# Halving the filler products of TensorE's first waits, and a newly written order of issue, in a block-recurrent attention and feed-forward kernel

## Chip, cores and metric

The kernel runs on one NeuronCore of one Trainium2 chip, as a single launch. The metric is device time in microseconds (us). The engines are named as the profile names them: PE (TensorE matmul), PEld (TensorE weight load), DVE (VectorE), ACT (ScalarE), POOL (GpSimd) and SP (SyncE, which here only issues DMAs).

## What is computed

```python
# x: (8, 8, 512, 64), state: (8, 8, 32, 64), both f32
scores = scale * x @ state.T                  # per batch and head, 512 x 32
xread  = softmax(scores, -1) @ state          # 512 x 64
scores2 = scale * state @ x.T                 # 32 x 512
sread  = softmax(scores2, -1) @ x             # 32 x 64
a = concat([xread, sread], axis=2)            # (8, 8, 544, 64)

t = a.transpose(0, 2, 1, 3).reshape(4352, 512)
h = t @ w_in                                  # 512 -> 2048
g = h * erf(softplus(h))
out = g @ w_out                               # 2048 -> 512
```

## The kernel before

Everything is f32. A batch (block) `b` has 512 tokens (its x rows) and 32 state rows. The feed-forward part is run in two halves `u` of the 2048 hidden columns. The product of the attention weights with the state and then with `w_in` is regrouped: state times `w_in` is formed first (`mixed`, L836), and the attention weights are applied to that (`first_product`, L935). First and second products use seven-product schemes in place of eight, some of them twice nested (L935, L1019, L1255), whose sums run on DVE (L975, L986, L1237) and whose copies out of PSUM run on ACT (L947, L1265).

Block 0 is done apart, while the weights still arrive (functions ending in `0`): eight heads of x are loaded by four DMAs (`load`, L395), transposed (`turn`, L410), scored (`score`, L436), the scores turned (`turn_score`, L442), and a softmax runs on DVE and ACT (L461 to L471) for two groups `g` of four heads. The attention weights are turned back (`turn_a`, L446) and copied into the tile `aT` (`either("ta0")`, `either("ta1")`). `mixed0` (L586) forms state times `w_in` for one or two column groups, and its result is copied into the tile `m`. `first0` (L604) is the first product of block 0: two matmuls of 128x512 that sum over the two groups, `es` 0 and 1; for block row `i` = 0 of the first half they were already two operations of one matmul each (`split`), for the others one operation of two. `second0` (L629) is the second product. In the same stretch the weights are loaded into three `raw` buffers and converted by `convert`: two ACT passes (L548, L550) and three DVE passes (L552, L554, L556) for each pair of 128-column groups. After a `raw` buffer is free, SP loads the next pair into it.

Query tiles for the later blocks are loaded by `load_xq` (16 DMAs of 64 KB, L93), transposed on DVE (L684) and scored on PE (L692). The x rows are loaded by `load_x_static` (4 DMAs of 256 KB, L783).

Nothing is issued as it is written. Each piece of work is recorded by `op(engine, cost, at, go, reads, writes, ...)`, with a cost in us, a due time `at`, and for DMAs a transfer time `pipe` and a time to landing `land`. At the end `emit` takes, for each engine, an order written out by hand as numbers in the table `ORDER` (number k is the k-th operation recorded for that engine). It computes when each would begin by the costs, and issues them all sorted by that begin. `in_order` then ties each engine to that order. So what stands on an engine one behind the other is set by `ORDER`; the costs, `land` and `pipe` only set how the engines' lists are merged. An engine never overtakes in its own list: an operation that waits holds up all behind it.

`either(name, ...)` puts a small copy on DVE if its name is in the set `BY_VECTOR`, and on ACT if not.

`spare_products(name, n, at)` records `n` filler products: `warm` (L115) multiplies the 128x128 identity by itself into a PSUM bank that is not in use. Their results are never read. They lie between the operations of block 0, where TensorE would wait. Including the eight at the very start (operation 0, `begin0`), the program has 78 of them. Each is recorded in the profile as two MATMUL rows, as every f32 product that is not a transpose is.

```python
def spare_products(name, n, at):
    op(PE, 0.112 * n, at, lambda: warm(bank(name)[:, 0:P], n), [], [name])
```

Of the kernel before, what the change touches and what calls it, by code (L numbers as in the profile page):

```python
# [17 lines left out]
def kernel(  # L18
# [21 lines left out]
    P = 128  # L40
# [99 lines left out]
    def op(engine, cost, at, go, reads=(), writes=(), table=None, land=0.0, pipe=0.0):  # L140
# [14 lines left out]
        x0 st s00 ta0 m001 m010 m011 m020 u1 m120""".split())  # L155

    def either(name, cost, out, in_, at, reads, writes):
# [3 lines left out]
        else:  # L161
# [4 lines left out]
            0 8 5 1-3 6 4 9 7 10 12 15-16 21 17 22 18 25 19 13 23 11 24 14 26-29 20 31 33 32 53 30  # L166
            45 68 52 44 69 71 34 54 36 35 37 70 39 47 38 40 55 57 56 48-49 73 58-59 50 41 61 42 46
            51 63 72 43 76-77 92 78 74 79 81 80 62 82 85 60 83 75 84 88 64 87 89 93 86 65 90 66 94
            91 67 95 101 96-97 105 102 106 98 130 129 103-104 107-108 132 131 109 133 110-111 134
            136 112 135 138-139 113 137 140 114-115 141 117 99 143 116 118 142 100 121-122 119  # L170
            123-124 120 144 146 125-127 176 148-149 152-153 128 179 178 150-151 180 154 177 181 183
            182 155-156 186 160-161 187 185 157-158 184 188 162-163 189 159 145 190 147 164 191 193
            168-169 165 224 170-171 223 166-167 226 225 195 227 172-174 230 196-198 228-229 199 233
            200 232 175 201 234 211 202 207 203 231 212 235 204 192 237 208 236 194 205-206 209 238
            240 210 270 213-216 271 217-218 272-273 242 239 243-244 274 245 219-220 275 250 276
            221-222 251 277 246 258 254 252 280 255-256 247-248 281 278-279 282 253 241 283 249 259
            284-285 257 287 286 260 262 317 263-264 261 320 265 319 318 266-268 289-290 269 291 321
            292 288 324 322 297-298 323 327 293 326 325 299 328 300-302 294-295 329 303 305-306 330
            296 304 332 331 333 309-310 363 307 364 311-312 308 366 335 365 367 313-314 336 315 370
            334 368 316 369 373 342 372 343 345 344 374 371 338 346 337 376 347 339 348 375 340 356  # L180
            341 357 405 358 349 359-360 407 351 361 353 362 406 350 352 384 409 386 385 355 388 387
            354 377 389 408 390 378-379 411-412 381 380 382 398 413 383 414 400 391 402 410 415 393
            392 417 394-395 416 418 399 401 433-434 397 396 439-440 437 441 435 403 442 436 404 438
            443 423 444-446 419 424 421 448 447 420 431 463 422 429 464 427 466 432 425 467 465 430
            426 468 428 470 453 449 473 469 451 472 471 474 454 450 475-476 452 459 457 460 477-478
            455 458 507 461 456 462 508 510 479 486 509 511 487 480 512 488 482 514 490 481 513 483
            489 517 516 484-485 492 518 515 491 493 520 500 495 519 522 521 501 494 502 497 496
            551-552 503-504 553-554 499 506 558 505 555 530 498 556 523 531-532 524 557 561 560 525
            559 533 562 527 534 563 535 526 564 528 565-566 536 529 595 544 537 545 539 547 546 538
            548 597 549 541 540 598 550 596 574 599 542 576 543 602 578 600 567 575 579 577 568 601  # L190
            569 605 603 570 606 571 607 572 604 580 608 588 573 609-610 581 589 591 590 583 640 639
            582 592 642 593 585 594 641 643 584 618 586-587 619-621 611 644 613 646 615 622 645 623
            612 649 648 647 614 624 650 632 617 652 616 651 625 633 654 653 634 627 635 683 636 626
            637 629 628 685-686 684 630 687 631 638 655 688 662 656 690 657 663-665 692-693 666 689
            694 659 658 668 691 660 695 667 696 676 697-698 661 727 678 677 669 679 670 672 680 671
            681-682 673 730 674 728 731 675 729 732 706 699 707 709 708 700 710 733 711 701-702 734
            703 735 737 704 712 736 738 720 705 739 713 740 722 715 721 724 723 741-742 714 725 716
            771 717 726 718 773-774 750 719 752 751 775 743 772 776 754 753 778 745 744 777 755 780
            756 781 747 782 779 746 748 783-784 764 749 765 757 766-767 759 758 761 760 768 762-763
            770 785 769 786-788 792 789 793 795 791 794 790 799 796 801 800 797-798 803 802 806  # L200
            804-805 808 807 813 809-810 815 814 816-817 811-812 818-819""",
        ACT: """
            0-3 5 4 11-12 6 13 7 14 8 31 16 15 9 17-18 55 20 10 56 19 32-34 36 38 21-22 37 39 24 23
            35 40-41 25-26 43 42 44-45 27-28 47 50 49 46 48 29 51 61 53 52 54 57-60 65 64 66-67
            94-95 68 102 104 103 70 107 69 106 71 98-99 72 77 63 96-97 79 76 73-74 78 80 75 86-87 81
            100 84 101 85 82 135 83 134 136-137 90 138-139 105 91 30 92 88 93 89 149 145 112 108 113
            151 150 62 152-153 158 142 140 159-160 141 161 146 109 143 162 155 147 157 144 165 163
            171 154 172 156 164 166 148 167 176 175 174 114 168 173 110 169 186 170 188 177 189 187
            190 182 195 179-180 111 115 178 197-198 196 192 200-201 194 118 184 199 191 193 203 202
            208 181 209 116 211 210 213 212 121 183 117 119-120 204 223 205 185 225 206 224 226 207  # L210
            227 232 215 123 234 214 122 219 216 233 217 125 124 126 235 229 236 245 127 130 218 230
            238 231 246 131 228 247 249 248 239 221 250 220 129 260 240 237 241-244 128 261-262 222
            253-254 256 263-264 133 252 269 132 251 271-272 268 270 274 266 273 265 275-276 255
            282-283 267 285 277 286 258 287 284 278 297 279-281 257 259 299 290 298 291 289 288 300
            293 301 306 308 294 292 309 307 310 305 303 313 304 302 311 295 322 321 319 314 312
            315-316 320 317 344 296 318 346 345 347 324 348 353 329 355 354 350 356 330 351 323 332
            325 331 326 352 327 349 333 357 361 360 328 339 358-359 362-363 340 334 341-342 364 335
            337 365 343 386 336 371-372 374 373 338 366-367 375 388 369-370 368 381 389 382 376 392
            377 390 379 378 387 393 384 399 401 394 391 395-396 383 385 380 402 397-398 405 403 407
            406 400 404 414 412-413 415 417 408-411 419 418 420-421 426 423 425 428-429 427 432 424  # L220
            422 430 433 431 434-436 439 437 442 441 440 463 438 416 465 448 443 464 466 449 467 472
            445 444 451 446 470 473 450 468 474-475 477 469 452 447 453 476 458 488 480 471 479 454
            485-486 478 487 459 481 509 482-483 455-456 461 460 510-511 484 512 462 457 494 513 518
            489 495 519 490 520 514 521 497 496 492 516 524 522 498 491 517 526 523 532-533 531 493
            525 515 534 504 555 499 527-528 500 505 529 506-507 530 502 501 557 508 556 540 558 541
            543 559 564 503 535 561 566 536 560 537 567 563 538 568 544 562 542 571 570 565 569 539
            572 550 573-574 579 578 580 545 577 551 575 546 576 552 601 553 548 554 603-604 547 586
# [3 lines left out]
            663 636 631 664 669 662 670 642 665 671 637 672 643 666 693 667 644-645 638 668 640 639  # L231
            646 695 641 696 694 678 673 697 679 681 674 698 701-702 675-676 680 682 699 704 677 703
            705 700 706 688 708-709 683 707 710 689 711 691 712 684 715 690 713 718 716-717 685-686
            692 739 714 687 724 741 725 742 740 727 719-720 743 726 748 745 750 744 746 751 722 747
            754 749 721 728 752-753 755 723 734 756-757 729 758-759 730 735 760 732 736 731 737 733
# [1255 lines left out]
    for i in range(2):  # L1491
        first0(0, i, "h%d" % i, 19 + 1.8 * i, split=not i)
# [220 lines left out]
```

## Time and profile before

| what | value |
|---|---|
| median of 3 runs | 710.77 us (709.85 to 713.2) |
| the profiled execution: its time / its span | 709.41 us / 707.6 us |
| TensorE clock granted, mean | 0.998 |
| HBM moved | 92.88 MB, mean 131 GB/s |
| DMA share, 10 to 20 / 20 to 30 / 30 to 40 us | 0.93 / 0.36 / 0.96 |

How to read it. The span runs from the first to the last instruction of the profiled execution; its time has 1.8 us more around it. Busy time of PE is a union of matmul rows whose ends are modelled, so PE can be reported as 100% busy when its rows are issued at a slower pace; start-to-start times within a group of like products are the safer reading. Since a filler product is a matmul as any other, the busy share of PE counts it as work. In the timeline a row is a run of like instructions on one engine: start, length, engine, line, operation, out<-in, and how many; brackets hold the idle time before it and what ended that.

### The profile page before, as it was taken

What the parts mean: (1) busy time and instruction counts of PE and PEld (TensorE: products, weight loads), DVE (VectorE), ACT (ScalarE), POOL (GpSimd) and SP (SyncE); (2) the same over time, 40 slices, a digit from 0 to 9 for tenths busy, and PEclk for the clock granted to TensorE, in tenths of its full rate; (3) what the DMA queues carried; (4) which work ended last, traced back from release to release, by engine and by line L of the source; (5) the groups of instructions that cost most, each with busy time, mean ns of one, the idle gap of its engine ahead of it and who ended that gap; (6) DMA issues with size and microseconds to landing.
All of it is one profiled execution on the core that took longest, in us unless ns stands there. A gap on an engine that the chain in (4) does not pass through costs nothing.

```text
span 707.6 us, 13386 instructions
## 1 busy us (share of the span) xinstructions
PE 698.9 (99%) x5259; PEld 592.3 (84%) x5259; DVE 593.9 (84%) x989; ACT 468.3 (66%) x847; POOL 85.6 (12%) x93
## 2 busy tenths in 40 slices
PE   9999989999999999999999999999999999999997
PEld 8734658787878878899999788898989898998996
DVE  5799989999999999797945589597969596959797
ACT  5797887868679393757335574759584757575832
POOL 0001010100111010000100100002242124122222
PEclk9999999999999999999999999999999999999999
DMA  8675969595969855413542720216385425555275
GB/s 272 159 195 127 224 183 198 186 222 160 220 162 253 257 204 153 151 74 82 119 112 79 236 67 31 68 16 113 46 128 63 95 24 104 75 60 61 30 135 105
DMA packets 133742, 92.88 MB, mean 131 GB/s; under 512 B 93744, under 2 KB 120752, under 8 KB 133168
## 3 DMA queue, kind: packets, MB, share of 16 engines
q1 hardware_dynamic: 114336, 61.88, 32.2%
q0 software_dynamic: 18800, 29.63, 22.7%
q8 instruction: 41, 0.67, 0.4%
q10 hardware_dynamic: 544, 0.52, 0.2%
q14 instruction: 21, 0.17, 0.1%
HBM read 50.86 MB, written 41.16 MB: 130 GB/s over the span
## 4 chain that ended last, share of the span: by engine, by line
PE 83%; DVE 6%; SPq 2%; issue 1%; DMA 0%; ACT 0%; DVEq 0%
PE o L1255 28%; PE h L935 17%; PE o L1019 17%; PE at L935 7%; PE o L1438 3%; PE h L1389 2%; PE h L836 2%; PE at L836 2%; SPq L93 2%; PE o L629 1%; DVE ring L986 1%; PE at L1389 1%; PE at L798 1%; DVE ring L1187 1%; PE h L692 1%
## 5 line engine op out<-in xcount | busy, mean ns | idle before, releaser
L947 ACT COPY ring<-h 128x512 f32<-128x512 f32 x120 | 68.8, 586 | 82.0 <-PE h L935 72.6
L935 PE MATMUL h<-aT,m 128*128 128x256 f32 x360 | 91.4, 380 | 0.0
L975 DVE TENSOR_TENSOR ring<-ring 128x1024 f32<-128x1024 f32 (+1 forms) x64 | 73.0, 1153 | 18.0 <-ACT ring L972 17.8
L1019 PE MATMUL o<-w_out,ring 128*128 128x256 f32 x320 | 77.2, 381 | 0.0
L957 ACT ACTIVATE ring<-ring 128x512 f32<-128x512 f32 x120 | 71.8, 631 | 6.9 <-DVE ring L953 3.9
L935 PEld LDWEIGHTS h<-aT,m 128*128 128x128 f32 x360 | 65.4, 190 | 9.4 <-issue 1.0
L986 DVE TENSOR_TENSOR ring<-ring 128x1024 f32<-128x1024 f32 x60 | 72.7, 1219 | 0.3
L1255 PE MATMUL o<-w_out,w_in 128*128 128x128 f32 x512 | 69.6, 277 | 0.3 <-DVE ring L1280 0.2
L1019 PEld LDWEIGHTS o<-w_out,ring 128*128 128x128 f32 x320 | 59.9, 190 | 10.8 <-issue 1.2
L1255 PEld LDWEIGHTS o<-w_out,w_in 128*128 128x128 f32 x512 | 64.1, 192 | 3.3 <-DVE oo L1270 1.1
L1255 PE MATMUL o<-w_out,ring 128*128 128x128 f32 x480 | 64.5, 276 | 0.0
L1255 PEld LDWEIGHTS o<-w_out,ring 128*128 128x128 f32 x480 | 61.1, 192 | 2.3 <-DVE ot L1270 0.4
L972 ACT ACTIVATE ring<-ring 128x1024 f32<-128x1024 f32 (+1 forms) x64 | 62.8, 1004 | 0.2
L1019 PE MATMUL o<-raw,ring 128*128 128x256 f32 x240 | 58.8, 382 | 0.0
L1019 PEld LDWEIGHTS o<-raw,ring 128*128 128x128 f32 x240 | 44.9, 190 | 10.7 <-issue 3.4
L1255 PE MATMUL o<-raw,ring 128*128 128x128 f32 x360 | 49.1, 275 | 0.0
L1255 PEld LDWEIGHTS o<-raw,ring 128*128 128x128 f32 x360 | 45.6, 192 | 1.8 <-issue 0.8
L1255 PE MATMUL o<-raw,xT 128*128 128x128 f32 x320 | 42.1, 276 | 0.0
L1255 PEld LDWEIGHTS o<-raw,xT 128*128 128x128 f32 x320 | 39.0, 192 | 1.4 <-issue 0.8
L1175 POOL DMA_DIRECT2D out_dram<-oo x16 | 23.6, 1548 | 116.7 <-DMA out_dram<-oo 93.9
L629 PE MATMUL o<-w_out,ring 128*128 128x512 f32 x64 | 31.2, 602 | 0.8 <-DVE ring L620 0.7
L935 PE MATMUL at<-aT,sx 128*128 128x256 f32 x120 | 31.0, 381 | 0.2 <-DVE ring L949 0.2
(270 smaller groups left out, 1418.4 us busy)
## 6 DMA issues: line engine op xcount, KB each, us to landing
x<-in_x_dram SPq DMA_DIRECT2D x30, 256.0 KB, 5.0
xq<-in_x_dram SPq DMA_DIRECT2D x112, 64.0 KB, 2.5
out_dram<-oo SPq DMA_DIRECT2D x10, 512.0 KB, 3.4
raw<-in_moe_w_in_dram SPq DMA_DIRECT2D x8, 512.0 KB, 6.2
raw<-in_moe_w_out_dram SPq DMA_DIRECT2D x4, 1024.0 KB, 7.5
raw<-in_moe_w_out_dram POOLq DMA_DIRECT2D x8, 512.0 KB, 4.7
raw<-in_moe_w_in_dram POOLq DMA_DIRECT2D x8, 512.0 KB, 5.4
kept_a<-aT SPq DMA_DIRECT2D x8, 512.0 KB, 4.8
```

Source lines behind the costliest of these rows:

```text
L629: nc.tensor.matmul(out=bank("o%d" % r), lhsT=gT[g][:, i, P * r:P * r + P], rhs=w_out[:, GF * g + i, :], start=(made_of[r] == 1), stop=(mad ...
L836: nc.tensor.matmul(out=bank(names[k])[Ns * p:Ns * p + Ns, :], lhsT=st[r, b, q], rhs=of_group[2 * u + j][r, :, i, :], start=True, stop=True)
L935: nc.tensor.matmul(out=out_[:, i], lhsT=x_[:, q:q + P], rhs=y_, start=(start and i == 0), stop=(i == 1), skip_group_check=not start)
L947: op(ACT, 0.5, t, lambda: nc.scalar.copy(out_(), view(bank(name))), [name], w)
L957: op(ACT, 0.53, t, lambda: nc.scalar.activation(out=part(splane, k), in_=part(hplane, k), func=ACTF.Softplus), area(hplane, ks=[k], os=[o] ...
L972: op(ACT, 0.085 + 0.875 * share, at + n, lambda s_=s_: nc.scalar.activation(out=s_, in_=s_, func=ACTF.Erf), [], area(splane, ks=[k], os=os ...
L975: op(DVE, 0.065 + 1.075 * share, at + n + 1, lambda s_=s_, h_=h_: tt(s_, s_, h_, op=ALU.mult), area(hplane, ks=[k], os=os), area(splane, k ...
L986: op(DVE, 1.14, at + k, lambda k=k, x_=x_, y_=y_, how=how: tt(get("h", k), get(*x_), get(*y_), op=how), area(v[x_[0]], ks=[x_[1]]) + area( ...
L1019: nc.tensor.matmul(out=view(name)[:, h], lhsT=lhs[:, i, :], rhs=weight_of[n]()[:, u, i, :], start=(start and h == 0 and i == 0), stop=(h = ...
L1175: op(GP, 1.2, t, lambda: nc.gpsimd.dma_start(out=quad(r, c), in_=one(v), accum_op=ALU.add), every(*v), [("out", b, r, c)], land=3.0, pipe=2.0)
L1255: nc.tensor.matmul(out=out_[:, Q2 * k:Q2 * k + Q2], lhsT=lhs[:, k, i], rhs=rhs[:, i], start=first, stop=(k == len(ns) - 1 and i == 1), ski ...
L1389: nc.tensor.matmul(out=bank(bk)[:, P * i:P * i + P], lhsT=x_[:, i, k], rhs=y_[:, k], start=(start and i == 0 and k == 0), stop=(i == GF - ...
```

## The change

Five edits are made together.

1. The cost that the planner is told for one filler product goes from 0.112 to 0.224 us, and there are fewer of them: 14 become 6 and 3 become 2 in `begin0`; the eight groups of 6 become eight groups of 3. With the two groups that stay (3 and 2) and the eight at the start, 78 products become 45.
2. `first0` of the first half is split by `es` for block row `i` = 1 too: one more operation of PE, the same matmuls. The first two block rows are now four operations.
3. The planner is told later landings: `land=4.0` in place of 2.5 for the x rows of a later block, and `land=6.0` for its query tiles. No DMA is added or removed.
4. Ten names stand in `BY_VECTOR` as before, but other ones: `st`, `ta0`, `m001`, `m010` and `u1` go to ACT, `x2`, `ta1`, `m000`, `m021` and `m121` to DVE.
5. All five lists of `ORDER` are written anew.

```diff
     BY_VECTOR = set("""
-        x0 st s00 ta0 m001 m010 m011 m020 u1 m120""".split())
+        x0 x2 s00 ta1 m000 m011 m020 m021 m120 m121""".split())
...
     ORDER = {
         PE: """
-            0 8 5 1-3 6 4 9 7 10 12 15-16 21 17 22 18 25 19 13 23 11 24 14 26-29 20 31 33 32 53 30
...
+            0-1 5 2-3 6 4 8-9 7 15 22-23 17 16 12 24-25 18 10-11 19 13-14 20 26-30 21 34 33 45 31-32
...
         SP: """
-            1 0 2 5-10 4 21 3 18 17 11-12 14 13 22-23 15 24 19 16 20 25-26 28 27 29 31-32 35 34 33
...
+            1 0 2 5-6 8 7 9-10 19 24 4 17 3 20 11 18 12 14 13 15 21 23 22 16 25-26 28 27 31 29 34 32
...
     def spare_products(name, n, at):
-        op(PE, 0.112 * n, at, lambda: warm(bank(name)[:, 0:P], n), [], [name])
+        op(PE, 0.224 * n, at, lambda: warm(bank(name)[:, 0:P], n), [], [name])
...
-            spare_products("o%d" % g, 3 if g else 14, 12.6 + 5 * g)
+            spare_products("o%d" % g, 2 if g else 6, 12.6 + 5 * g)
...
-            op(SP, 3.0, 60, lambda: load_x_static(1), [], ["x"], pipe=5.2)
+            op(SP, 3.0, 60, lambda: load_x_static(1), [], ["x"], land=4.0, pipe=5.2)
...
             op(SP, 9.6, scored_at + 1, lambda: load_xq_static(b + 1),
-               [], ["xq"] + ["xq%d" % i for i in range(NI)], pipe=7.6)
+               [], ["xq"] + ["xq%d" % i for i in range(NI)], land=6.0, pipe=7.6)
...
-            op(SP, 3.0, at + 1, lambda: load_x_static(b + 1), [], ["x"], pipe=5.2)
+            op(SP, 3.0, at + 1, lambda: load_x_static(b + 1), [], ["x"], land=4.0, pipe=5.2)
...
-    for k, at in enumerate((12.7, 13.4, 14.1, 15.3, 16.5, 17.3, 20.6, 21.2)):
-        spare_products("o%d" % (2 + k // 4), 6, at)
+    for k, at in enumerate((12.7, 13.4, 14.1, 15.3, 16.5, 17.3, 18.5, 20.6)):
+        spare_products("o%d" % (2 + k // 5), 3, at)
...
-        first0(0, i, "h%d" % i, 19 + 1.8 * i, split=not i)
+        first0(0, i, "h%d" % i, 19 + 1.8 * i, split=True)
```

What the new lists say of the start, read from the built programs: between the second scoring (L436, group 1) and the first matmul of `first0`, TensorE had 62 filler products and now has 32; the other work of that stretch is the same (one `turn_score`, two `mixed0` of one column group, two `turn_a`). The two fillers that stood first after the eight now stand behind the fourth transpose of x. On DVE the second row maximum of the state softmax (L481) moves from before the second group's first maximum to behind the first group's normalisation. On SP, in the stretch around 75 us, the sixteen DMAs of block 3's query tile now stand ahead of the two DMAs that save block 0's attention weights (L880), and were behind them.

More of the change, by code (lines that the diff above doesn't have):

```diff
@@ L171 @@
[L171 to L175, printed above, removed]
@@ new lines @@
+            145 147 126-127 177 128-129 179-180 178 184 181 149-151 182-183 152 186-187 157 153
+            158-159 154 160-161 165 188 185 166 189 162-163 167 191 146 155 164 156 148 190 169 168
+            170-171 194 192 172 196-198 224 199 173 225-227 174 204 231 228 175 205 229 176 200 234
+            206 201 233 230 235 207 202 208 203 232 236 209 237 210-211 238 193 212 195 213-214 239
+            241 215 271 243 216 274 217-219 244 273 220 245 272 240 275 221 278 276 242 246 222-223
@@ new lines @@
+            510 462 461 463 512 487 480 515 489 488 490-491 513 482 481 483 518 492 514 517 484 519
+            516 493 485 521 520 501 486 503 494 522-523 496 552 495 502 504 497-498 555 505 499
+            553-554 507 506 556 531 500 533 532 559 534-535 524 557-558 525-526 561 528 527 562
+            536-537 529 563 560 545 564-565 547 566-567 530 546 538 549 548 539-540 596 542 541 599
+            543 550 598 551 603 575 597 544 600 577 568 601 576 578 569 602 579 570 606 572 571 604
+            581 605 607 574 573 580 608-609 582 589 611 610 590-591 640 584 583 585 642 593 592 586
@@ new lines @@
+            704 712 701 703 741 705 721 740 706 723 722 714 743 742 725 724 716 715 772 718 774 773
+            717 719 775 727 779 776 720 751 726 777-778 753 744 752 754 745 755 746 780 782 748 783
+            756 747 784-785 757 749 781 765 750 766 758 768 760 759 767 762 761 769 764 763 770 786
+            771 787-790 793 791 795 792 794 797 800 796 802 801 803-804 799 798 807 806 805 809 808
+            814 811 810 816 812 815 818 817 813 819-820""",
+        ACT: """
+            0-1 4 2 5 3 11-12 7 13 6 14 8 31 16 15 10 32 17-18 9 55 20 19 56 33-34 37 39 38 40 21-22
+            36 23-24 35 42 41 25-26 44 43 29 45 27-28 30 47 50 46 49 48 53 61 51-52 54 58 57 59 64
+            60 65-68 102-103 106 94 107 95 70 69 98 71 105 104 99 72 77 96-97 74 78-79 82 75-76 80
+            73 100 86-87 81 63 84 83 85 90 101 134-135 91 137 136 138 92-93 88 139 149 62 150 89 145
+            112 151 110 113 111 152 142 146 143 153 108-109 158 160 140 159 147 161 141 164 157 156
+            154 162 155 172 165-166 171 144 148 163 174 173 175-176 167 186 119 168 115 187 117 188
+            169 114 170 189 118 190 195 182 116 197 196 178 177 179-180 198-199 183 200 202 194 192
+            120 193 208 191 184 201 181 121 209 203-204 123 213 210 212 211 125 185 205 122 206 223
+            207 219 124 216 224-226 126 215 214 227 232 217 127 234-235 228 238 229 236 233 237 220
+            128 240 231 239 246 221 230 245 218 241 248-249 247 250 242 260 129 132 130 243 222 131
+            244 262 252 261 251 253 263 133 254 264 269 256 271-272 270 266 273 257 276 274 277 268
+            255 265 258 275 267 285 284 282 278 283 279-280 286-287 297 259 288 290 299 289 281 298
+            291 300 293 301 306 308 292 295 309 307 303 302 305 311 304 310 313 294 314 312 315-317
+            296 322 318-321 344-345 324 346-347 323 329 325 348 353 350 330 351 331 327 354-355 326
+            332 356 333 359 352 349 357 360 358 361 339 362 328 340 363 334 342 386 364 335 341 365
+            337 336 343 338 371-373 387 374 366-367 369 368 375 388-389 381 370 376 391 377 392 390
+            378-379 394 393 395-396 383 382 397 399 401 398 384 402-403 380 385 400 404-405 407 406
+            408 412 414-415 409-411 413 417 419-420 418 422 421 426 424 423 428 425 429 432 427 430
+            433-434 441-442 431 439 435 440 436 416 463 437 465 438 464 448 466 443 449 451 467 472
+            469 474 444 452 468 446 450 445 475 470 473 477 471 478 476 479 458 480 447 481 453 486
+            485 482 488 454 459 487 483-484 509 460 456 461 455 511 457 510 462 494-495 512 489 513
+            518 515 490 497 492 517 496 520 519 514 521 516 523 493 491 524 498 504 522 525-527 505
+            533-534 532 499 531 528 506-507 500 529 555 502 530 503 501 556 508 557 540 558 535 542
+            541 559 564 536 543 538 566 563 537 567 565 560 570 544 562 539 568 572 545 569 550 580
+            571 577 561 578 573 551 601 579 546 574-576 552 548 553 603 547 602 604 549 554 586-587
+            581 605 610 607 582 589 612 606 588 584 613 608 583 609 616 590 611 585 596 614 617 615
+            591 618-619 592 625-626 623 597 620 624 621 598-599 622 647 594 600 593 649-650 648 595
+            627 651 656 628 632-633 653 635 652 658 636 654 630 659 655 662 629 660 634 657 631 661
+            664 663 672 671 669 637 665 638 642 666 643 667 670 645 668 639-640 693 646 644 695 641
+            678 696 679 694 697 702 680-681 673-674 704-705 698 703 701 708 676 700 699 675 710 707
+            682 688 706 677 709 711-712 689 683 713 715 714 718 717 690 684 716 739 686 691 740-741
+            685 687 742 692 724 745 725 743 719 727 748 720 744 726 747 750 722 751 721 728 754 746
+            752 756 723 755 749 753 734 757 729 758-759 730 760 735-736 732 731 737 733 761 738 762
+            764 763 766 765 767 769 771 768 772 774 773 770 776 775 777 781 779 778 780""",
@@ L288 @@
+            42 41 47 39 44 50 49 45 48 52 46 51 53 57 55 54 59-60 56 62 64 61 63 65 58 67 70 66
+            71-72 68-69 78 77 73-76 80-81 79 82-83""",
     }
```

173 lines of the change are left out of this document (65 added, 108 removed), and 3 rows, old and new, of the table ORDER.

## The prediction

> **What bounds the kernel now.** I read four views: the page's busy times, the windows by stage, the timeline of PE in the first 27 us, and the waits.
>
> The page and the windows (columns: window, its length, busy us and instructions of PE, PEld, DVE, ACT and POOL, granted clock, DMA share, GB/s):
>
> ```profile
> PE 698.9 (99%) x5259; PEld 592.3 (84%) x5259; DVE 593.9 (84%) x989; ACT 468.3 (66%) x847; POOL 85.6 (12%) x93
> 10.00:27.00 17.00, 17.00 (x195) 16.06 (x177) 11.80 (x26) 9.70 (x17) 0.00 (x0) 1.00 0.76 213
> 27.00:64.00 37.00, 35.86 (x152) 14.86 (x151) 35.57 (x51) 34.33 (x43) 0.00 (x0) 1.00 0.64 156
> 64.00:200.00 136.00, 134.03 (x962) 102.22 (x961) 131.71 (x227) 107.11 (x188) 13.07 (x21) 1.00 0.78 195
> 200.00:690.00 490.00, 489.80 (x3763) 439.06 (x3762) 399.20 (x654) 309.27 (x584) 68.31 (x63) 1.00 0.47 107
> ```
>
> From 200 us on PE alone is the bound: 489.80 of 490 us, with DVE at 81%. From 27 to 200 us PE and DVE are both full (97% and 96% up to 64 us, then 99% and 97%). From 10 to 27 us PE is full too, but not with work. Its timeline there:
>
> ```profile
> 10.29 3.39 PE L115 MATMUL o<-ident 128*128 128x128 f32 x28
> ...
> 15.10 5.62 PE L115 MATMUL o<-ident 128*128 128x128 f32 x48
> 20.66 0.45 PE L586 MATMUL h<-w_in,ring 64*32 64x128 f32 x16
> 21.04 3.62 PE L115 MATMUL o<-ident 128*128 128x128 f32 x30
> 24.49 0.60 PE L446 MATMUL o<-ident,ring 128*128 128x128 f32 x4
> ```
>
> L115 is the filler. From 15.10 on, other engines wait for PE while it works on fillers. From the waits of the first 80 us (us in total, times, longest), of DVE and then of ACT:
>
> ```profile
> DVE aT L160 <- PE o L446: 3.0, 1, 3.0
> DVE m L160 <- PE h L586: 1.8, 1, 1.8
> ```
> ```profile
> ACT ring L487 <- PE o L446: 5.0, 1, 5.0
> ```
>
> L446 (`turn_a`, group 0) started at 24.49, but its input, the L471 of 17.63, was ready at 18.33. L586 at 20.66 had its weights at 14.52 (L556) and its banks at 15.91 (copy L160). So both were kept by fillers queued ahead of them, L446 by 6.2 us.
>
> **Edit 1 and the new PE list (the stretch 10.29 to 26.70).** One product costs PE its start-to-start time: 28 rows from 10.29 to the next start at 13.52 are 14 products in 3.23 us, 48 rows from 15.10 to 20.66 are 24 in 5.56 us: 0.231 each. The stretch ends where `first0` starts, 26.70. Its 16.41 us are 62 x 0.231 = 14.3 of fillers and 2.1 of work (L442, two L446 at 0.44 each, two L586 at 0.38). Nothing there is a wait. With 32 fillers PE needs 7.4 + 2.1 = 9.5 us, so `first0` could start at 19.8.
>
> Do its inputs allow that? DVE worked without a wait on PE from 9.05 to 19.44, 10.39 us, for 19 instructions. By the new list it has the same 19 to do (the L481 stands later, one copy `m` is another of the same size), then L471 of group 1, L552, one copy `m` and the copy `ta1`: 0.69 + 0.69 + 0.28 + 0.69 = 2.35 by their busy rows. That ends at 21.8, and `ta1` is what the second half of `first0` reads; the first half starts 0.87 earlier (26.70 to 27.57), at 20.9. `ta0`, for the first half, is now on ACT behind the L550 that ended at 20.15: with its 0.58, 20.7, and up to 0.6 less as the L466 ahead of it no longer waits behind an L481. So `first0` starts between 19.8 and 20.9. I take 20.5, nearer to the inputs' end: **gain 6.2 us** (5.8 to 6.9). The next group of fillers, 6 products at 30.94, becomes 3: another 0.7 on PE if nothing waits there, 0 if DVE does. The maximum L481 that moves back is read by the exponential L487 (25.18 before), whose result PE first reads at 64.80 (L500): 39 us of cover.
>
> Does it last through 27 to 200 us, where DVE is full as well? DVE loses its 3.02 and 1.77 us of waits, and by the new list has done one L552 (0.6 from start to start) more when it comes to the L554 that was at 26.65: 5.4. The exchanged copies give it x2 0.69, ta1 0.69, m000 0.28, m021 and m121 0.42 each, and take st 0.42, ta0 0.69, m001 and m010 0.28 each, u1 0.52: 0.3 more work, on an engine that is full. So DVE carries 5.1, and PE up to 6.9 + 0.7 = 7.6. PE decides after 200 us, but can't run ahead of its operands before: I keep the **6.2**, ends 5.1 and 7.6.
>
> **Edit 2.** The same four matmuls; the two halves that are split today started 0.87 apart, an unsplit pair holds PE 1.72 to 1.81 (the pairs at 32.71 and 44.59). Nothing, hidden or not.
>
> **Edits 3 and 5: the later landings.** One query landing cost time:
>
> ```profile
> DVE xq L684 <- DMA xq<-in_x_dram: 2.5, 2, 2.3
> ...
> PE h L692 <- DVE xq L684: 1.6, 1, 1.6
> ```
>
> DVE stood 2.27 us before 99.78 and 0.25 before 101.34, queued in front of the sums of `mixed` (L847), and PE 1.58 us before 102.16. The sixteen DMAs were issued from 82.53 on, behind the save L880 (1.22 us on SP, 512 KB) that they now pass; behind them the save is now later, and nothing soon reads it. The gain is at most the 2.3 of DVE, at least 0, and below nothing if another DMA is late in its place. It comes to 1.6 if PE alone counts. I take 1.4.
>
> **New waits elsewhere.** All lists differ up to the end. From 200 to 690 us the old order left 0.2 us of PE idle, so the new one can only equal or worsen that; one late landing of the size just seen is 1.6. I take 0.6 for the 620 us. The tail behind the last matmul: the last two stores held SP 1.11 us (from 703.85); the new list has three behind the last sums in place of two: 0.55 more at most, 0.2 taken.
>
> **Sum.** -6.2 - 1.4 + 0.6 + 0.2 = **-6.8 us**. On the profiled execution: 709.41 to 702.6. That one lies 1.4 us below the median of 710.77, and I predict the median: **704.0 us**.
>
> **A rule that speaks against it.** PE ran slower at first: its eight first products took 0.444 us each (0.78 to 4.33), the next two 0.99 us, and a row of L115 lasted 421 ns there and 275 ns from 10.3 us on, although the granted clock reads 1.00 in both. So a half rate that the clock column doesn't show ends between 5 and 10 us.
>
> The Trainium skill, "TensorE: Matmul & The Clock Gate", section "What's actually happening", says that the clock falls to half after an idle window of some 3.4 us and that a busy one lifts it. By that rule the fillers are what holds the clock, and taking them off is a risk only where PE would idle for such a window.
>
> In my sum PE has 9.5 us of work in the 10.2 from 10.29 to 20.5, so it idles 0.7 in all, in pieces. In the first 10 us it idled 0.8.
>
> **Rivals.**
> (a) *The cold clock (slower).* Two fillers are moved from 4.33 to behind the transposes, and the transposes wait for x's DMAs, so the half rate might last. If PE runs the whole stretch at half rate, 9.5 us become 19.0: `first0` starts at 29.3, 2.6 later than before, and its four products of 0.87 lose 3.5 more: 2.6 + 3.5 - 1.4 + 0.6 + 0.2 = +5.5, 716.3. It turns to a loss when over two thirds (6.2 of 9.5) run at half. For it: the slow start. Against it: after 10 us no gap of PE is near that long. 0.05.
> (b) *DVE decides up to 200 us, and landings stay late.* DVE's 4.8 of waits less 0.3 of copies, and nothing for the landing, less 0.8 of new waits and tail: -3.7, 707.1. With one new wait of 1.6: 708.7. For it: DVE at 97% from 27 to 200. Against: PE is as full. 0.2.
> (c) *It gives nothing (711).* That would be so if the time from 20 us on were set by the weights' arrival. DMA share from 30 to 40 us is 0.96; but from 20 to 30 it is 0.36, as SP waited 4.9 us for DVE's L556 to free a buffer before its load at 29.21, and that L556 comes some 5 us earlier. 0.07.
> (d) *All fillers count*: 33 x 0.231 = 7.6, and 2.3 of the landing, no new waits: -9.9, 700.9. PE's 99% speaks for it, DVE's against. 0.06.
>
> **Chances.** The forecast (702 to 706) 0.62, (a) 0.05, (b) 0.2, (c) 0.07, (d) 0.06. A measurement tells apart about 0.5%, 3.6 us. Faster by more: (under 707.2): the forecast, (d) and half of (b): 0.78. Within it: the rest of (b) and (c): 0.17. Slower: (a): 0.05. The range leaves out (a), (c) and the far side of (d): 700.5 to 708.7.
>
> **What would show it.** In the changed profile: L115 about 90 rows in place of 156; the first L604 row at 20 to 21 us (later than 22: DVE or ACT held it; rows of 421 ns behind 10 us: (a)); no DVE wait on L446 or L586 of over 1 us; no wait of L684 of over 1 us near 95 us; the last matmul 6 to 8 us earlier, with no more than 1 us of PE idle between 70 and 690 us. I am wrong if `first0` starts early and the last matmul does not: then waits after 30 us have eaten it.

## The result, and the profile after

| | before | changed |
|---|---|---|
| median (range), 4 runs each | 710.35 us (709.85 to 713.2) | 702.68 us (701.84 to 703.79) |
| ratio, 95% interval | | 0.9885 [0.9853, 0.9916] |
| the profiled execution: its time / its span | 709.41 / 707.6 us | 703.79 / 702.0 us |
| PE busy | 698.9 us | 692.0 us |
| `first0` starts | 26.70 us | 20.78 us |
| last matmul row starts | 702.86 us | 697.12 us |

The change makes the kernel faster by 7.7 us from median to median, and by 5.6 us between the two profiled executions (the profiled one of the changed kernel is the slowest of its four). All that follows is read from profiles, so it accounts for the 5.6; the other 2 us lie within the spread of the runs. (A second set of runs of the same kernel, e7 below, gave 704.34 us and 0.9926.) In the changed kernel every line number from L167 on is one higher than before.

The page's busy times and the windows by stage of the changed kernel (window, length, busy us and instructions of PE, PEld, DVE, ACT and POOL, clock, DMA share, GB/s):

```profile
PE 692.0 (99%) x5193; PEld 583.9 (83%) x5193; DVE 593.1 (84%) x989; ACT 471.8 (67%) x849; POOL 85.6 (12%) x93
10.00:27.00 17.00, 15.99 (x140) 11.51 (x139) 16.53 (x30) 15.39 (x24) 0.00 (x0) 1.00 0.78 217
27.00:64.00 37.00, 36.35 (x190) 15.37 (x192) 35.70 (x58) 32.33 (x43) 2.80 (x4) 1.00 0.71 179
64.00:200.00 136.00, 133.54 (x927) 102.82 (x916) 130.69 (x223) 107.11 (x183) 10.79 (x18) 1.00 0.79 203
```

From 10 to 27 us DVE and ACT are now as full as PE (97% and 91%, and were 69% and 57%): the start is no longer PE's alone. The two matmul rows of each of 33 fewer fillers account for the 66 rows that PE has less (5193 against 5259). PE's timeline, then two rows of DVE's:

```profile
14.78 2.27 PE L115 MATMUL o<-ident 128*128 128x128 f32 x18
17.20 0.66 PE L447 MATMUL o<-ident,ring 128*128 128x128 f32 x4 [0.15 <-DVE ring L472]
17.70 1.28 PE L115 MATMUL o<-ident 128*128 128x128 f32 x10
19.61 0.66 PE L447 MATMUL o<-ident,ring 128*128 128x128 f32 x4 [0.64 <-DVE ring L472]
20.11 0.83 PE L115 MATMUL o<-ident 128*128 128x128 f32 x6
20.78 3.60 PE L605 MATMUL h<-aT,m 128*128 128x512 f32 x8
```
```profile
18.87 0.69 DVE L472 TENSOR_TENSOR ring<-ring,z1b 128x512 f32<-128x512 f32 x1
20.35 0.68 DVE L160 COPY aT<-o 128x512 f32<-128x512 f32 x1
```

Both `turn_a` (L447) now wait for DVE, for 0.15 and 0.64 us, where the first had stood behind fillers for 6.2 us. `first0` starts at 20.78, while DVE still copies `ta1` for its second half (to 21.03): inputs and PE have come together.

To see whether the gain lasts I compare, for each kernel, when PE has done the same work: all products but the fillers, weighted by 0.43, 0.216 and 0.111 us for 512, 256 and 128 columns. The table gives how far each profiled execution is ahead of before, in us. It can swing by about 1 where the order of products differs.

| ahead at (us of before) | 50 | 100 | 110 | 140 | 200 | 700 |
|---|---|---|---|---|---|---|
| changed | 6.4 | 5.9 | 8.2 | 8.3 | 5.6 | 5.7 |
| e1: old counts, new lists | 1.5 | 1.0 | 3.4 | 3.4 | 3.5 | 2.9 |
| e2: new counts, old lists | 5.7 | 6.4 | 7.9 | 7.9 | 7.9 | 7.9 |
| e3: changed, no fillers | 5.5 | 5.0 | 7.3 | 7.3 | 7.4 | 6.9 |
| e4: before, query ahead of the save | 0.5 | -11.5 | -9.3 | -9.2 | -9.2 | -9.2 |
| e5: changed, state save before x | 6.1 | 5.0 | 7.3 | 7.3 | 2.5 | 2.6 |
| e6: before, 21 fillers behind the first 8 | 4.6 | 5.3 | 5.9 | 5.9 | 5.9 | 6.0 |
| e7: changed, again | 5.4 | 4.9 | 7.2 | 7.3 | 5.1 | 5.2 |
| e8: changed, save and receive early | 6.3 | 5.5 | 7.8 | 7.8 | 7.0 | 7.1 |
| e9: e2 again | 5.3 | 6.0 | 4.1 | 4.3 | 4.3 | 4.3 |

The changed kernel has three steps: about +6 at the start, +2.3 around 103 us (the query landing), and -2.7 between 140 and 200 us. From 200 us on nothing changes. The last loss stands in the waits and the timeline of the changed kernel (lines from several engines):

```profile
PE o L1020 <- DVE ring L976: 2.2, 1, 2.2
```
```profile
123.97 5.98 SPq L784 DMA_DIRECT2D x<-in_x_dram  x4
131.47 0.34 SPq L763 DMA_DIRECT2D kept_t<-xT  x1
...
139.02 0.71 DVE L715 STREAM_TRANSPOSE xT<-m 128x512 f32<-128x512 f32 x1 [2.67 <-ACT m L549]
139.66 1.18 DVE L976 TENSOR_TENSOR ring<-ring 128x1024 f32<-128x1024 f32 x1
140.89 2.43 PE L1020 MATMUL o<-w_out,ring 128*128 128x256 f32 x10 [2.24 <-DVE ring L976]
```

DVE's L715 overwrites `xT`, which the save `kept_t` (L763) still reads. The line view of L763 in this stretch says when the save landed:

```profile
DMA to landing us min/median/max: 7.5/7.5/7.5
```

131.47 + 7.5 = 138.97, and L715 starts at 139.02. The bracket names ACT's L549, which happened to end at the same time; but L715 does not need it: in e3 below L715 starts at 137.20 and that L549 at 139.29. It is the DMA that ended the wait, and in e7 the profile names it. Behind L715 stands L976 in DVE's list, and PE waits for its sum. Without the wait L715 would have begun at 136.35, so the save has 4.9 us to land. In the kernel before, the same save landed in 3.3 us and was issued ahead of the x tile (139.06 against 139.47):

```profile
139.06 0.32 SPq L762 DMA_DIRECT2D kept_t<-xT  x1
139.47 2.79 SPq L783 DMA_DIRECT2D x<-in_x_dram  x3
```

The new SP list puts the x tile's four DMAs in front of it.

### The profile page after: what moved, and what is told of

Its sections match the earlier page's. It is cut to its first block, busy times and chain, and to the rows that moved or that the text cites. A ratio compares the mean times of both kernels' runs of the same rounds, so it can differ in the third digit from the quotient of the medians.

```text
span 702.0 us, 13245 instructions
## 1 busy us (share of the span) xinstructions
PE 692.0 (99%) x5193; PEld 583.9 (83%) x5193; DVE 593.1 (84%) x989; ACT 471.8 (67%) x849; POOL 85.6 (12%) x93
## 4 chain that ended last, share of the span: by engine, by line
PE 81%; DVE 9%; ACT 2%; issue 1%; DVEq 0%; ACTq 0%
PE o L1256 30%; PE h L936 17%; PE o L1020 15%; PE at L936 7%; PE o L1439 4%; PE h L1390 2%; PE at L837 2%; PE h L837 2%; PE at L799 1%; DVE ring L976 1%; PE at L1390 1%; DVE ring L987 1%; PE h L693 1%; DVE xT L721 1%; DVE xT L715 1%
## 5 line engine op out<-in xcount | busy, mean ns | idle before, releaser
L976 DVE TENSOR_TENSOR ring<-ring 128x1024 f32<-128x1024 f32 (+1 forms) x64 | 73.0, 1152 | 26.6 <-ACT ring L973 26.2
L1020 PE MATMUL o<-w_out,ring 128*128 128x256 f32 x320 | 77.7, 382 | 2.2 <-DVE ring L976 2.2
L1020 PEld LDWEIGHTS o<-w_out,ring 128*128 128x128 f32 x320 | 59.9, 190 | 16.0 <-DVE ring L976 4.2
L1020 PE MATMUL o<-raw,ring 128*128 128x256 f32 x240 | 58.6, 381 | 0.0
L1020 PEld LDWEIGHTS o<-raw,ring 128*128 128x128 f32 x240 | 44.9, 190 | 8.3 <-issue 1.7
L936 PE MATMUL h<-sy,m 128*128 128x256 f32 x120 | 30.9, 380 | 0.1
L936 PE MATMUL at<-sy,sx 128*128 128x256 f32 x120 | 31.0, 381 | 0.0
```

The source lines that it names most:

```text
L936: nc.tensor.matmul(out=out_[:, i], lhsT=x_[:, q:q + P], rhs=y_, start=(start and i == 0), stop=(i == 1), skip_group_check=not start)
L976: op(DVE, 0.065 + 1.075 * share, at + n + 1, lambda s_=s_, h_=h_: tt(s_, s_, h_, op=ALU.mult), area(hplane, ks=[k], os=os), area(splane, k ...
L1020: nc.tensor.matmul(out=view(name)[:, h], lhsT=lhs[:, i, :], rhs=weight_of[n]()[:, u, i, :], start=(start and h == 0 and i == 0), stop=(h = ...
```

## The experiments

Every kernel here computes the whole result; where fillers are taken out, only unread products go. Each set of runs has its own runs of before beside it: 710.45 us (7 runs) for the first four, 709.35 (14) for the next three, 709.18 (12) for the last two.

**e1 and e2: counts and lists apart.** e1 is the changed kernel with the old counts, e2 the kernel before with the new ones.

```diff
 e1, in the changed kernel
-            spare_products("o%d" % g, 2 if g else 6, 12.6 + 5 * g)
+            spare_products("o%d" % g, 3 if g else 14, 12.6 + 5 * g)
-        spare_products("o%d" % (2 + k // 5), 3, at)
+        spare_products("o%d" % (2 + k // 5), 6, at)
 e2, in the kernel before
-            spare_products("o%d" % g, 3 if g else 14, 12.6 + 5 * g)
+            spare_products("o%d" % g, 2 if g else 6, 12.6 + 5 * g)
-        spare_products("o%d" % (2 + k // 4), 6, at)
+        spare_products("o%d" % (2 + k // 4), 3, at)
```

> The changed kernel with the old numbers of filler products (14 and 3, eight groups of 6), everything else as changed. Theory (the fillers themselves held the start): between the second scoring and first0 PE again has 62 x 0.231 + 2.1 = 16.4 us, so first0 starts at 9.6 + 16.4 = 26.0 (20.78 in the changed kernel), and 3 more products follow: 5 to 6 us lost for good, ratio to the kernel before 0.996 to 1.000. Rival (the new lists brought the gain, and the fillers lie in waits): first0 at 20.8 to 22.3, ratio under 0.992.

> The kernel before with the new numbers of filler products (6 and 2, eight groups of 3), its own lists of order kept. Theory: PE has 32 x 0.231 + 2.1 = 9.5 us from 10.29, so it could start first0 at 19.8; the old list of DVE still has an L481 and a copy ahead, and its L471 and copy ta0 end some 1.5 us behind 19.44: first0 at 20.9 to 21.4, 5.3 to 5.8 us gained, ratio 0.991 to 0.993 if the query landing stays late. Rival (the lists brought it): first0 later than 24, ratio 0.997 or more.

e1: 706.7 us, 0.9945 [0.9929, 0.9962]. e2: 703.02 us, 0.9891 [0.9873, 0.991]. PE's timeline in e1, then in e2:

```profile
17.30 4.73 PE L115 MATMUL o<-ident 128*128 128x128 f32 x40
21.86 0.60 PE L447 MATMUL o<-ident,ring 128*128 128x128 f32 x4
26.09 3.60 PE L605 MATMUL h<-aT,m 128*128 128x512 f32 x8
```
```profile
18.12 0.60 PE L446 MATMUL o<-ident,ring 128*128 128x128 f32 x4
19.82 0.66 PE L446 MATMUL o<-ident,ring 128*128 128x128 f32 x4 [0.43 <-DVE ring L471]
20.62 3.70 PE L604 MATMUL h<-aT,m 128*128 128x512 f32 x8
```

In e1 the fillers hold `turn_a` back again (it starts at 21.86, its input, DVE's L472, was ready at 18.40), and `first0` is 5.3 us later than in the changed kernel. In e2 it starts at 20.62, with the old lists and all other edits left out. So the counts give the start by themselves. (e2's ratio lies below the 0.991 expected, as the query landed in time for PE in its profile.) The lists and other edits with the old counts give about 1 us by 100 us and 2.4 at the landing, and keep both (the save `kept_t` landed in 4.1 us here, and PE did not wait at 140); that is why e1's ratio lies below the 0.996 that was expected. And the counts alone reach the changed kernel's ratio: there, what the lists add at 103 us, they take away at 140.

**e3: no fillers at all but the first eight.** This is the test of the cold clock.

```diff
-            spare_products("at0", 2, 9.2)
+            spare_products("at0", 0, 9.2)
-            spare_products("o%d" % g, 2 if g else 6, 12.6 + 5 * g)
+            spare_products("o%d" % g, 0, 12.6 + 5 * g)
-    spare_products("h0", 3, 10.7)
+    spare_products("h0", 0, 10.7)
-        spare_products("o%d" % (2 + k // 5), 3, at)
+        spare_products("o%d" % (2 + k // 5), 0, at)
```

> The changed kernel with no filler products but the eight at the start (37 fewer). Theory: what first0 reads now bounds it, so it starts at 20.3 to 20.8, and the time stays within 1 us of the changed kernel; matmul rows of 128 columns stay at 275 ns behind 10 us. Rival (the clock: fillers keep PE fast): rows of 421 ns in the stretch from 10 to 30 us, pairs of first0 matmuls further apart than 0.87 us, first0 later than 21.5, and 2 to 6 us lost.

702.41 us, 0.9886 [0.9867, 0.9904]: as fast as the changed kernel. But its windows show that the clock did fall:

```profile
10.00:14.00 4.00, 1.04 (x20) 0.60 (x20) 3.81 (x9) 3.45 (x8) 0.00 (x0) 1.00 1.05 375
14.00:16.00 2.00, 0.68 (x16) 0.23 (x16) 1.97 (x5) 1.20 (x2) 0.00 (x0) 0.54 0.67 98
16.00:20.00 4.00, 1.58 (x6) 1.18 (x7) 3.83 (x10) 3.69 (x6) 0.00 (x0) 0.50 1.04 311
20.00:24.00 4.00, 4.00 (x9) 1.89 (x8) 3.60 (x6) 3.98 (x7) 0.00 (x0) 0.50 0.58 117
24.00:26.00 2.00, 2.00 (x13) 0.63 (x15) 1.63 (x2) 1.14 (x2) 0.00 (x0) 0.90 0.67 124
```

Its timeline has two long waits ahead of the slow products:

```profile
12.03 0.45 PE L587 MATMUL h<-w_in,ring 64*32 64x128 f32 x16 [2.33 <-DVE w_in L557]
...
17.12 1.12 PE L447 MATMUL o<-ident,ring 128*128 128x128 f32 x4 [2.33 <-DVE ring L472]
20.44 5.57 PE L605 MATMUL h<-aT,m 128*128 128x512 f32 x8
```

`first0` starts no earlier than with fillers (20.44 against 20.78), since DVE sets it, and its four products take 5.57 us in place of 3.60. At 30 us e3 is ahead of before by 4.4 us, the changed kernel by 6.0 and its repetition e7 by 5.6: up to there the cold clock costs 1.2 to 1.6 us. Little of it lasts: at 110 us e3 stands at 7.3, against 8.2 and 7.2. The two then part by the other wait: in e3 `kept_t` landed in 4.0 us, and PE did not wait at 140. So the fillers that the change takes out cost time, and what those that it leaves are worth does not show in the total.

The Trainium skill, "TensorE: Matmul & The Clock Gate", section "What's actually happening", gives an idle window of some 3.4 us as the condition for the half rate. The trace agrees that the clock falls to half, but it fell here with no gap of PE longer than 2.33 us, PE being busy for 1.04 of the 4 us before. The measurement decides: a mostly idle stretch was enough.

**e4: the query's DMAs ahead of the save, in the kernel before.** It tests the reason that the prediction gave for the late landing.

```diff
-            1 0 2 5-10 4 21 3 18 17 11-12 14 13 22-23 15 24 19 16 20 25-26 28 27 29 31-32 35 34 33
+            1 0 2 5-10 4 21 3 18 17 11-12 14 13 22-23 15 24 19 16 20 25-26 28 27 31 29 32 35 34 33
```

> The kernel before with one step of SP's list moved: the sixteen DMAs of block 3's query tile ahead of the save of block 0's attention weights (L880, L881). Theory (the save held the query tile): DVE's wait at L684 falls from 2.3 us to under 1, PE's of 1.6 us at L692 is gone, and the curve of work against time gains 1.5 us at 102 us and keeps it. Rival (POOL's burst of loads and stores from 87.7 us on held the last pieces): L684 still waits 1.5 us or more, no gain.

718.54 us, 1.0113 [1.0096, 1.013]: slower by 8.1 us, which no theory expected. The waits of DVE and PE between 60 and 110 us:

```profile
DVE aT L751 <- DMA kept_a<-aT: 10.0, 1, 10.0
PE at L811 <- DVE sn L804: 9.7, 1, 9.7
```

The save reads the tile `aT` of block 0, and DVE's transpose L751 overwrites it. Behind the sixteen query DMAs (10.73 us on SP, from 80.52) the save is issued at 91.30 instead of 81.19, L751 waits 10 us for it, and PE 9.7 us behind that. So something does soon need what the save holds up: not a reader of the copy, but the next writer of its source. At 97 us the granted clock falls to 0.50, until 107, and that costs more (four matmuls of L935 take 2.07 us, 1.13 in the kernel before). In the changed kernel, with the same swap, DVE had no such wait: there the sixteen are issued from 75.20 to 84.48 and the save at 84.52, 6.8 us earlier than in e4.

The query did gain by the pass. Its twelfth DMA landed at 91.8 us (99.7 in the kernel before, where the first L684 waited for it), and its last at 98.7 (101.2). DVE, held at L751 until 100.06, could not use that. The last three still landed only at 98.4 to 98.7.

What else differs in time is POOL's DMAs. In the kernel before, POOL issues six DMAs from 87.71 to 91.4 us, in the middle of the query's sixteen (82.53 to 99.45 with the waits between them), and in e4 likewise (86.56 to 90.2 within 80.52 to 91.25). In the changed kernel POOL's burst begins at 92.45, when the query is issued in full. In all five profiles with the old lists the last query DMA issued ahead of POOL's first weight load (L539) of this burst landed 3.8 to 5.2 us after its issue, and the next one 8.2 to 10.2 us after. The Trainium skill, "DMA: Bandwidth & Descriptors", section "Queues, rings and completion order", says that each DMA engine goes round its queues packet by packet; that fits pieces which land late while another queue is busy. No run here moved POOL's burst alone, so this is argued and not shown.

**e5 and e8: the save `kept_t` back in front of the x tile, in the changed kernel.** e8 also moves the receive (37) that hangs on the save one place up.

```diff
-            35 33 30 38 36 46 41 39-40 43 37 44 50 45 42 47 53 48 51 49 52 57 60 56 55 54 58-59 61
+            35 33 30 36 38 46 41 39-40 43 37 44 50 45 42 47 53 48 51 49 52 57 60 56 55 54 58-59 61
 e8
+            35 33 30 36 38 46 41 39-40 37 43 44 50 45 42 47 53 48 51 49 52 57 60 56 55 54 58-59 61
```

> The changed kernel with one step of SP's list moved: the four DMAs of an x tile (issued from 123.97 us) behind the save of the attention weights kept_t (L763, issued at 131.47). Theory (in the changed kernel's profile that save landed 7.5 us after its issue, at 138.93, because x's last piece, landing at 136.37, was ahead of it; DVE's L715 at 139.02 waited to overwrite what the save reads, and PE's 2.2 us at L1020 hung on it): the save lands within 4 us, L715 and L1020 wait under 0.5 us, the gain of 8.2 us at 110 us stays to the end, ratio to the kernel before 0.985 to 0.988. Rival (the wait only moves: x or the next query tile land later instead): another wait of PE of 1.5 us or more before 175 us, ratio 0.988 to 0.991.

> The changed kernel with two steps of SP's list moved: the x tile's four DMAs behind the save kept_t, as in the run before, and the four DMAs that bring it back (sc from kept_t, L768) ahead of the next query tile's sixteen (issued from 144.38 there). Theory (the 3.0 us of PE at L799 in the run before were the last of those four, which landed at 163.60 behind five DMAs that POOL issued from 154.92 on): they land before 152, PE waits under 0.5 us at L1020 and at L799, and the gain of 7 to 8 us at 110 us stays to the end: 2 us below the changed kernel, ratio 0.985 to 0.990. Rival (SP's and POOL's transfers only change places again): the query tile is late for L693 near 168 us, or another wait of 1.5 us or more appears.

e5: 705.08 us (9 runs), 0.9936 [0.9913, 0.9958]. The wait of L1020 is gone, since the save landed in 4.9 us, but one takes its place later, in PE's timeline:

```profile
163.74 1.10 PE L799 MATMUL at<-x,sc 128*32 128x64 f32 x64 [2.98 <-DMA sc<-kept_t]
```

That is the receive of `kept_t`. Its third piece was issued at 155.38 and landed at 158.99; the fourth, issued at 155.85 just behind the first weight load of a POOL burst (155.46), landed at 163.60. And the wait cost more than its 2.98 us. The next row of PE:

```profile
164.77 4.54 PE L1020 MATMUL o<-raw,ring 128*128 128x256 f32 x12
```

In the changed kernel twelve such matmuls take 2.86 us (at 163.32). The granted clock was 0.50 here, for 3.4 us. The wait and these 1.7 us make up 4.7 of the 4.8 us that e5 loses between 140 and 200 us. Its ratio lies above both ranges that were expected.

e8 takes both waits away: in its profile PE has no wait of over 0.3 us between 30 and 690 us, and it ends 7.1 us ahead of before (702.35 us). Its median is 704.28 us (7 runs), 0.9936 [0.9907, 0.9965]: no better than the changed kernel. The two waits are real, but the times of e8's runs lie between 701.66 and 707.41, and only one execution was profiled. Its three longest runs show a mean granted clock of 0.996 or 0.997, the four others 0.999 or 1.000 (3.4 us at 0.50 lower the mean by 0.002). That would fit a wait of PE with a cold clock behind it, as in e5; which one is not known.

**e6: the old lists with fewer fillers still**, 21 behind the first eight.

```diff
-            spare_products("o%d" % g, 3 if g else 14, 12.6 + 5 * g)
+            spare_products("o%d" % g, 0, 12.6 + 5 * g)
-        spare_products("o%d" % (2 + k // 4), 6, at)
+        spare_products("o%d" % (2 + k // 4), 2, at)
```

> The kernel before, its own lists, with no fillers in the two groups of begin0 (14 and 3) and eight groups of 2 in place of 6: 16 + 3 + 2 stay behind the first eight. Theory (below the new counts, first0's inputs bound the start and the clock starts to matter): first0 at 20.0 to 20.7, as with the new counts; if the granted clock falls under 1.00 anywhere in 10 to 30 us, 0.5 to 1.5 us are lost behind it, ratio 0.988 to 0.992. Rival (PE's queue still bounds the start): first0 before 19.6, ratio under 0.988.

704.09 us, 0.9918 [0.9898, 0.9937], with `first0` at 21.76. A window and a row of PE's timeline:

```profile
10.00:15.00 5.00, 3.81 (x70) 2.86 (x68) 4.81 (x9) 4.42 (x10) 0.00 (x0) 1.00 0.91 328
```
```profile
5.32 1.12 PE L424 MATMUL h<-ident,ring 128*64 128x128 f32 x8
```

The clock stayed at 1.00 in the records with PE busy 76% of that window. The row at 5.32 took 0.66 us before: the half rate of the first microseconds lasted longer in this execution, past 6.37 us (the twelve matmuls behind it took 1.74 us against 1.53), and put it back by 0.7 us at 10 us. PE then waited 0.90 and 0.80 us for DVE's L471. So `first0` came later than the 20.0 to 20.7 expected, and fewer fillers than the change has give nothing: DVE sets the start.

**e7 and e9: the changed kernel and e2 once more**, no edit; e9 ran on another chip than e2.

> The changed kernel as it is, once more, on the same chip. If PE's wait of 2.2 us near 141 us belongs to its lists, it is there again with 1.5 us or more. If it was that execution's order of DMA packets, it is under 0.5 us, and the profile lies 1.5 to 2.5 us lower, near 700 us of span.

> The kernel before with the new numbers of filler products and its own lists, once more, on the same chip as the run beside it. If the lists gain nothing over the counts, its ratio is that of the changed kernel or lower, 0.989 to 0.993, with no wait of PE over 1.2 us between 30 and 690 us.

e7: 704.34 us (6 runs), 0.9926 [0.9907, 0.9945]. Its waits of PE and DVE between 100 and 150 us:

```profile
PE o L1020 <- DVE ring L976: 1.8, 1, 1.8
DVE xT L715 <- DMA kept_t<-xT: 2.2, 1, 2.2
```

The new wait came back, and here the profile names the DMA (7.0 us to landing). But e1 and e3 have the same order and nearly the same offsets (the save 7.5 us behind the first x DMA, POOL's last two DMAs from 2.75 us ahead of it), and there it landed in 4.1 and 4.0 us. The lateness begins ahead of the save: the third x DMA held SP for 3.93 us in the changed kernel and 2.98 in e7, against 2.27 in e1 and 2.76 in e3, and the fourth, issued behind it, landed in 7.4 and 6.9 us, against 4.3 and 4.4. The list takes the slack away; whether the wait comes is decided by landings that vary from one execution to the next.

e9: 703.21 us (6 runs), 0.9922 [0.9905, 0.9938]. Its waits of PE and DVE between 60 and 150 us:

```profile
PE h L692 <- DVE xq L684: 2.1, 1, 2.1
DVE xq L684 <- DMA xq<-in_x_dram: 3.1, 1, 3.1
```

In e2 the same kernel's L684 had waited 1.1 us and PE not at all; no wait of PE over 1.2 us was expected. With the old lists PE's wait for this landing was 1.6 us (before), 0 (e2), 1.0 (e6, where the profile names ACT) and 2.1 (e9); in all six profiles with the new lists it is gone. In e9 the clock fell behind the wait, in windows of the same columns as above:

```profile
94.00:97.30 3.30, 1.20 (x13) 0.80 (x17) 2.65 (x5) 1.53 (x2) 0.00 (x0) 1.00 0.16 27
97.30:100.70 3.40, 3.40 (x19) 1.47 (x9) 3.40 (x7) 1.56 (x4) 0.00 (x0) 0.50 0.25 96
```

From L692 to the second L935 behind it e9 takes 4.13 us and e2 2.68: another 1.5 us lost. In the changed kernel, behind its wait of 2.2 us, the clock stayed at 1.00.

**Not tried:** the split of `first0` alone, the exchanged copies of `BY_VECTOR` alone, the later landings told to the planner alone, and POOL's burst moved alone.

## Why the prediction was right, and where it was wrong

The forecast was 704.0 us, and 702.68 came out: right in sign and nearly in size. Step by step, in the profiled execution:

- **Start, 6.2 predicted: 5.9 measured.** `first0` began at 20.78 (20.5 predicted, ends 19.8 and 20.9). DVE's copy `ta1` ended at 21.03, a little earlier than the 21.8 worked out. e1 and e2 show that it comes from the counts. DVE's waits on the two kept-back products (3.0 and 1.8 us) and ACT's of 5.0 are gone.
- **It lasts through 27 to 200 us, as said.** e2 stands at 5.7 at 50 us and at 6.4 at 100 us: DVE at 97% did not take the gain back, and the first part of rival (b), that DVE decides up to 200 us, falls.
- **The query landing, 1.4 predicted: 2.3 measured, right in place and only half right in reason.** The prediction held that the query gains by passing the save, and that "nothing soon reads it". e4 shows that the pass does bring the landing forward (the last DMA by 2.5 us, the twelfth by 7.9), but that in the old order it costs 8 us: it is not a reader that comes soon but L751, which overwrites the source. In the changed kernel, where the save is issued 6.8 us earlier than in e4, that wait does not come. That POOL's burst comes later there is a second reason, which the prediction did not have and no run took apart.
- **New waits, 0.6 predicted: 2.7 measured** by the table, 2.2 of it PE's wait at L1020. This is the term that was mis-sized. The prediction looked for one late landing of 1.6 and took less than half of it; the new SP list made a dependence tight (4.9 us for a save that took 7.5) that had been slack. The sign "no more than 1 us of PE idle between 70 and 690 us" failed by this wait alone. That the slack would go could have been seen beforehand: SP's new list puts four 256 KB loads ahead of a save whose source DVE overwrites soon after. That the save would be late could not: in e1 and e3 it was not.
- **Tail, 0.2 predicted: 0.1 measured** (from the last matmul's start to the end of the span, 4.78 to 4.90 us).
- **Sum.** -5.9 - 2.3 + 2.7 + 0.1 = -5.4, against 5.6 between the spans, within the swing of the table. Two errors, of 0.9 and 2.1 us, partly cancelled. That is luck, as both terms hang on landings that vary from one execution to the next; the start is what the prediction had right by its reasons. The median came out lower than this since the profiled execution of before lies 0.9 us under its median and that of the changed kernel 1.1 us over its own.
- **Rival (a), the cold clock,** did not occur at half the count (granted 1.00 from 10 to 27 us). It is real at none (e3), where it costs 1.2 to 1.6 us by 30 us, little of it in the end, and makes no loss against before, as the rival's 5.5 would be. In e4, e5 and e9 the clock fell behind waits later in the kernel, which no rival had.
- **Rival (c), nothing gained,** falls with the result. **Rival (d), all fillers count,** falls too: e3 and e6 take more of them away, and `first0` starts at 20.44 and 21.76, against 20.78.

What stays open: why the landings of `kept_t` (4.0 to 7.5 us in one order) and of the query vary between executions, and what the longest runs of e5 and e8 wait for. The new counts with the old lists reach what the whole change reaches (0.9891 and 0.9922 in e2 and e9, against 0.9885 and 0.9926 for the change), and no kernel was measurably better. So, added to the new counts, the other edits together have no measurable worth, with a gain and a loss of over 2 us each. With the old counts they are worth 3.8 us (e1, 0.9945).

## What to carry to other kernels

Filler work in an engine that never overtakes costs what it delays and no more: count it up to the moment when the next input is ready, and take out what lies beyond. To take out the rest gained nothing here, and let the clock fall. When an order is written anew, list for each save which instruction next overwrites its source, and how long the save then has to land; a move that brings a load forward can hold up a chain that has nothing to do with it. A landing that is late in one profile may be on time in the next run of the same kernel, so look at two before pricing it. And a wait of TensorE of 2 to 3 us can cost more than its length, when the clock falls behind it (e5, e9).

## What the runs showed of the hardware that was not expected

- TensorE's granted clock fell to 0.50 after a stretch in which PE was busy for 1.04 of 4 us, with no gap over 2.33 us (e3). The shares of 0.54 in 14 to 16 us and 0.90 in 24 to 26 put the fall at about 14.2 and the return at about 24.4 us, some 4 us after dense work began at 20.44.
- It also fell behind single waits of 2.1 us (e9) and 2.98 us (e5), each time for 3.4 us, and of 9.7 us (e4), for 10.2 us. Behind the changed kernel's wait of 2.2 us it did not. PE was busy for 1.20 of 3.30 us (36%) ahead of the fall in e9, and for 1.66 of 3.00 (55%, 137 to 140 us) in the changed kernel, so the length of the wait alone does not decide.
- The half rate at the very start, which the clock column does not show, ended at different times in kernels that begin alike: a row of eight matmuls took 0.66 us at 5.32 in one and 1.12 us in another (e6). It put PE back by 0.7 us at 10 us.
- The same 7.5 us between the first x DMA and the save `kept_t` gave landings of 4.0, 4.1, 7.0 and 7.5 us (e3, e1, e7 and the changed kernel).
- An SP DMA of the query issued just ahead of a 512 KB weight load of POOL landed in 3.8 to 5.2 us, the next one, just behind it, in 8.2 to 10.2 us (before, e2, e4, e6, e9).
